# Batch 1's second FFN product in seven half products for eight

## The chip, the cores and the metric

The kernel runs on one core of a Trainium2 chip. A core has five engines with a queue of instructions each: TensorE (PE in the profile) multiplies matrices, VectorE (DVE) and ScalarE (ACT) work element by element, GpSimd (POOL) does so more slowly and issues most loads, SyncE (SP) issues stores. The metric is device time in microseconds (us) of one execution; lower is better. The median of three runs before the change is 284.22 us (284.15 to 285.25).

## The reference

Eight batches of eight heads go through an attention in which 32 global tokens see all 544 tokens and each of the 512 local tokens sees the global ones and a window of 32 to each side. The result, with the heads side by side, goes through an FFN of 512 to 2048 to 512 with a GELU (x times the sigmoid of 1.702 x).

```python
s_g = scale * np.matmul(q_g, k_all.transpose(0, 1, 3, 2))
out_g = np.matmul(sm(s_g), v_all)
mask = np.abs(pos[:, None] - pos[None, :]) <= window
s_ll = np.where(mask, scale * np.matmul(q_l, k_l.transpose(0, 1, 3, 2)), -1e9)
s_l = np.concatenate([scale * np.matmul(q_l, k_g.transpose(0, 1, 3, 2)), s_ll], axis=-1)
out_l = np.matmul(sm(s_l), np.concatenate([v_g, v_l], axis=2))
x = attn_out.transpose(0, 2, 1, 3).reshape(B * S, H * D)
h = x @ w_in
g = h * (1.0 / (1.0 + np.exp(-1.702 * h)))
return g @ w_out
```

## The kernel before

The order of the work on each engine is written out by hand: instructions go into an engine's queue in the order in which the program calls them, and each waits only for the data and the buffers that it needs. TensorE's order is the backbone. While it does the FFN of batch i it also does the attention of batch i+1 in between.

**Attention.** A quad is four heads; a batch has two, `a` and `c` (class `Wide`), and `a2`, `c2` are those of the batch after. `T` (or `Tk`, `Tq`) transposes keys and queries on VectorE, `kcopy`, `qcopy` and `ext` copy parts of them to where the score matmuls read them. `S(rnd)` are the score matmuls of one of two rounds (24 small ones), `X` the exponentials on ScalarE, `M` the multiplication with the mask, on VectorE or POOL. `U(0)` sums the rows, `U(1)` and `U(2)` multiply with the values, `Gm` does the global tokens. `R` turns the sums into reciprocals (transpose, reciprocal, transpose) and `XL` scales the result into `xL`, the FFN's input. `G`, or `keep_og`, `G_recip`, `G_mul` and `G_turn`, do the same for the global tokens.

**First product.** `h_step(i, fc)` makes one of 16 tiles of the hidden layer: four matmuls of 512 columns, then a GELU into `gT`. From batch 3 on (`h_some`) some tiles are made by `HPair` in seven products for eight.

**Second product.** For batches 0 and 1, `o_mm` adds up 16 matmuls of 512 columns for each of four tiles of 128 tokens, in sixteen parts of four matmuls. ScalarE copies each tile out of PSUM and SyncE stores it. From batch 2 on a class `Pair` does it by Strassen's scheme (in Winograd's kind): operands are cut in two along tokens, along the inner dimension and along the output, and seven products of sums of such parts stand for eight. `g_sums` makes the sums of `gT` on VectorE, `weight_sums` those of the weights (two of them in place, in `w_out_sb`). A `Pair` covers two tiles of 128 tokens; `mm(k)` is one half product of eight matmuls of 256 columns, into two PSUM banks `x` and `y`; `m3`, `z`, `zm`, `sub`, `evict`, `add` and `store` combine them:

```python
def sub(self):
    nc.vector.tensor_sub(self.zz, self.zz, self.x.rearrange("p (h m) -> p h m", h=2))
def evict(self):
    self.ob = moe.tile([128, 4, HM], F32, name="ob", bufs=3)
    on_act(self.ob[:, 1:3], self.x.rearrange("p (h m) -> p h m", h=2))
```

**PSUM.** Scores live in one pair of double banks (`spair`, `psS`, one buffer each), so `S` of a round waits until `X` has read the round before. Everything else (`hp`, `op`, `px`, `py`, `ov`, `og`) takes turns in four banks (`pbank`, `psP`).

**Loads.** Queries and keys (`load`), values (`load_v`) and the global tokens' rows (`load_g`) are issued on POOL's queue, in order with POOL's other work. Two sets of buffers hold queries and keys of two batches.

**Stages around the change.** Lines 960 to 1035: second product of batch 0 with batch 1's attention, then the start of batch 1's first product. Lines 1026 to 1054: the rest of batch 1's first product (with `weight_sums(0, 3, 4)` at 1028, and at 1029 to 1047 VectorE's work for batch 2's quads). `phase_o1` (1073 to 1114): batch 1's second product with batch 2's attention. Lines 1294 to 1318: batch 2's first product (with `weight_sums(1, 2)`). `phase_o(2)` (1116): batch 2's second product with batch 3's attention; then `h_some(3)`, `phase_o(3)` and so on.

Of the kernel before, what the change touches and what calls it, by code (L numbers as in the profile page):

```python
# [12 lines left out]
F32 = mybir.dt.float32  # L13
# [7 lines left out]
def kernel(  # L21
# [12 lines left out]
    nc = tc.nc  # L34
# [10 lines left out]
    NQ = B * 2  # L45
# [560 lines left out]
    def keep_og(q, ogs):  # L606
        on_act(ogs[:, q.u], q.st["og"][:, : D + 2])
# [69 lines left out]
    def h_weight_sums(g):  # L677
        w11, w12, w21, w22 = w_h[g]
        for t, x, y, op in zip(wh[g], (w11, w21, w11, w21, w12), (w22, w22, w12, w11, w22),
                               (ALU.add, ALU.add, ALU.add, ALU.subtract, ALU.subtract)):  # L680
            nc.vector.tensor_tensor(t, x, y, op)
# [77 lines left out]
    wsum = [wts.tile([128, FC // 2, HM], BF16, name="wsum%d" % k) if k in (0, 3, 4) else (b12, b21)[k - 1]  # L759
            for k in range(5)]  # L760

    def weight_sums(*ks):
        for k in ks:
            x, y, op = ((b11, b22, ALU.add), (b12, b22, ALU.subtract), (b21, b11, ALU.subtract),
                        (b11, b12, ALU.add), (b21, b22, ALU.add))[k]
            nc.vector.tensor_tensor(wsum[k], x, y, op)

    sums = {}

# [26 lines left out]
    class Pair:  # L796
# [37 lines left out]

        def zm(self):
            nc.vector.tensor_add(self.zz[:, 1], self.zz[:, 0], self.y[:, :HM])

        def evict(self):
            self.ob = moe.tile([128, 4, HM], F32, name="ob", bufs=3)
# [112 lines left out]
    for fc in range(4, FC):  # L952
        h_step(0, fc)
        if fc == 4:
            h_weight_sums(1)
        if fc == 12:
            h_weight_sums(2)
            h_weight_sums(4)

    def osteps(i, *sts):  # L960
        for tci, f4 in sts:
            o_mm(i, 4 * tci + f4)
# [10 lines left out]
    a.S(0)  # L973
    a.X(0)
    copy_vg1()
    c.Tk()
    c.Tq()
    c.ext()
    a.M(0)
    osteps(0, (0, 2), (1, 2))  # L980
    o_mm(0, 10, part=(0, 1))
    a.S(1)
# [40 lines left out]
    for kcs in ((0, 1), (2,), (3,)):  # L1023
        for fc in range(4):
            h_mm(1, fc, hps[fc], kcs)
    a.G()
    c.G()
    weight_sums(0, 3, 4)
    nq[2][0].Tk()
    nq[2][0].Tq()  # L1030
    transpose_g(4, 6)
    nq[2][0].ext()
    pt = spair()
    for fc in range(4, 8):
        h_mm(1, fc, bank(pt, (fc - 2) % 4), range(NKC))

    a, c = nq[2]
    for fc in range(FC):
        if fc == 11:
            c.Tk(False)  # L1040
            c.Tq(False)
            c.ext((0, 1, 2))
            c.kcopy(nc.vector.tensor_copy)
            c.ext((3,))
            c.qcopy(nc.vector.tensor_copy)
        if fc < 4:
            h_act(1, fc, hps[fc])
        elif fc in (4, 6):
            f = slice(fc, fc + 2)
            gelu(gTs[1][:, f, :], pt[1 - (fc - 4) // 2])  # L1050
        elif fc >= 8:
            h_step(1, fc)
        if fc == 13:
            a.S(0)

    def o_parts(i, *parts):
        for part in parts:
            o_mm(i, part)

    def loads_after(i):  # L1060
        if i + 2 < B:
            load_v(i + 2)
        if i == 1:
            load_g(8, NQ)
        if i + 3 < B:
            load(i + 3)

    def quads_of(n):
        if n < B and n not in nq:
# [3 lines left out]
    def phase_o1():  # L1073
        a, c = nq[2]
        a2, c2 = quads_of(3)
        a2.T()
        transpose_g(6, 8)
        a2.ext()
        a.X(0)
        a.M(0)  # L1080
        loads_after(1)
        o_parts(1, 0, 1, 2, 3, 4)
        a.S(1)
        a.X(1)
        a.M(1)
        o_parts(1, 5, 6, 7)
        c.S(0)
        c.X(0)
        a.UG()
        a.R()  # L1090
        c.M(0)
        o_parts(1, 8)
        c.S(1)
        c.X(1)
        a.XL(0)
        a.XL(1)
        a.G()
        c.M(1)
        o_parts(1, 9, 10, 11)
        a2.S(0)  # L1100
        a2.X(0)
        c.UG()
        loads_after(2)
        c.R()
        a2.M(0)
        c.XL(0)
        c.XL(1)
        o_parts(1, 12)
        a2.S(1)
        a2.X(1)  # L1110
        gelu_table()
        c.G()
        a2.M(1)
        o_parts(1, 13, 14, 15)

    def phase_o(i):
        b = i + 1
        a, c = nq[b]
        a2, c2 = quads_of(b + 1)
        p0, p1 = Pair(i, 0), Pair(i, 1)  # L1120
        ogs = att.tile([128, 2, D + 2], F32, name="ogs", bufs=1)
        late = a2 and i > 2
        exp_table()
        a.UG()
        c.S(0)
        a.R()
        g_sums(i, 7, 8, (0,))
        a.XL(0)
        wide = 2 < i < B - 1
        g_sums(i, 7, 8, (1,) if wide else (1, 2))  # L1130
        a.XL(1)
        g_sums(i, 7, 8, (3,))
        p0.mm(3, 4, 1)
        c.X(0)
        p0.m3()
        p0.z()
        if wide:
            g_sums(i, 4, 8, (2,))
# [36 lines left out]
        if a2:  # L1175
            c.XL(1)
            xg = G_mul(ogs, G_recip(ogs), nc.gpsimd)
            if i + 3 < B:
                load_v(i + 3, chunks=(2, 3, 4))
        p1.mm(3, 4)  # L1180
        p1.m3()
        p1.z()
        if c2:
            c2.Tk(False)
        else:
            c.XL(1)
# [104 lines left out]
        g_sums(i, 4, 6, (3,))  # L1291
        g_sums(i, 6, 8, (3,))

    for i in range(1, B):
        if i > 2:
            h_some(i)
        elif i > 1:
            for fc in range(FC):
                h_step(i, fc)
                if i == 2 and fc == 0:  # L1300
                    weight_sums(1, 2)
                if i + 1 < B:
                    c = nq[i + 1][1]
                    if fc == 1:
                        c.Tk()
                        c.Tq()
                        c.ext((3,))
                    if fc in (3, 5, 7):
                        c.ext(((3, 5, 7).index(fc),), on_act)
                    if fc == 9 and i + 2 < B:  # L1310
                        a2 = quads_of(i + 2)[0]
                        a2.T()
                        transpose_g(2 * i + 4, 2 * i + 6)
                        a2.ext()
                if fc in (4, 8, 12):
                    g_sums(i, fc // 2 - 2, fc // 2)
                if fc == 13:
                    g_sums(i, 6, 7)
        if i == 1:
            phase_o1()  # L1320
        elif i + 1 < B:
            phase_o(i)

    scores.close()
# [85 lines left out]
```

## Time and profile before

| what | value |
|---|---|
| median of three runs | 284.22 us |
| profiled execution's own time | 284.39 us |
| its span, first to last instruction | 282.7 us |
| TensorE's granted clock | 1.0 of full speed |
| TensorE busy | 277.0 us, 98% |
| VectorE busy | 227.6 us, 81% |
| ScalarE busy | 186.9 us, 66% |
| POOL busy | 112.3 us, 40% |

| stage (us of the span) | length | TensorE | VectorE | ScalarE | POOL |
|---|---|---|---|---|---|
| 52.86 to 65.60, batch 1, first product | 12.74 | 12.74 | 10.48 | 8.18 | 8.32 |
| 65.60 to 85.69, batch 1, second product | 20.09 | 20.09 | 15.54 | 15.71 | 14.43 |
| 85.69 to 99.51, batch 2, first product | 13.82 | 13.82 | 12.75 | 10.62 | 3.96 |
| 99.51 to 117.19, batch 2, second product | 17.68 | 17.68 | 16.25 | 11.12 | 7.24 |
| 130.61 to 148.35, batch 3, second product | 17.74 | 17.74 | 16.96 | 12.68 | 7.23 |

The profile is of one execution. A row of a timeline or of the chain of waits begins with its start and its length in us, then engine, line of the kernel, operation, and tile written <- tiles read; in brackets stands how long the engine was idle before and what ended that. PE is TensorE's matmuls, PEld its weight loads, which overlap with them. A group's row gives busy time and the mean length of one in ns; matmuls overlap in the pipeline, so their distance from start to start is less than their length. The view of waits gives, for an engine and line, what it waited for: us in total, times, longest. The chain of waits goes back from the last instruction to what released it each time.

### The profile page before, as it was taken

To read this page: it belongs to the slowest core of one execution; us is meant where nothing else is said; L and a number is where in the kernel's file an instruction comes from. 1 tells how busy PE (TensorE), PEld (TensorE's weight loads), DVE (VectorE), ACT (ScalarE), POOL (GpSimd) and SP (SyncE) were. 2 spreads that over 40 slices of the span, in tenths; PEclk is the share of its full clock that TensorE was granted. 3 is DMA by queue.
4 is the path that set the end of the run, shared out by engine and by line. 5 is a ranking of instruction groups with operands and counts; after the bars stand their busy time and mean duration, and the time that the engine had idled before them with its cause. 6 is when DMAs were issued, how large, how long until landed. Compare 5 with 4: busy or idle time off the path is not lost.

```text
span 282.7 us, 9018 instructions
## 1 busy us (share of the span) xinstructions
PE 277.0 (98%) x3787; PEld 185.5 (66%) x3787; DVE 227.6 (81%) x486; ACT 186.9 (66%) x319; POOL 112.3 (40%) x161
## 2 busy tenths in 40 slices
PE   8999999999999999999999999999999999999994
PEld 7554445544554488756886488757876589558884
DVE  7687368996689898989998899899997898586452
ACT  4847657577778785489756994689648961873331
POOL 8984550856936004970099206940080000000001
PEclk9999999999999999999999999999999999999999
DMA  7999996999999804994089807930023003300223
GB/s 207 155 191 205 204 174 84 146 218 157 165 172 175 151 2 58 93 156 90 12 108 131 148 5 91 86 70 2 20 62 74 2 2 77 74 2 1 58 54 113
DMA packets 59352, 28.24 MB, mean 100 GB/s; under 512 B 47472, under 2 KB 49776, under 8 KB 59312
## 3 DMA queue, kind: packets, MB, share of 16 engines
q0 software_dynamic: 51760, 17.83, 57.1%
q1 hardware_dynamic: 7120, 9.18, 11.8%
q8 instruction: 29, 0.48, 0.7%
q10 hardware_dynamic: 432, 0.66, 0.7%
q14 instruction: 11, 0.09, 0.1%
HBM read 36.31 MB, written 8.91 MB: 160 GB/s over the span
## 4 chain that ended last, share of the span: by engine, by line
PE 93%; DMA 2%; DVE 2%; ACT 1%; SPq 0%; issue 0%; DVEq 0%
PE hp L638 32%; PE px L821 13%; PE op L752 10%; PE py L821 9%; PE x L821 6%; PE s L560 6%; PE s L720 5%; PE ov L586 5%; PE s L638 3%; DMA early<-in_q_l_dram 2%; DVE xL L471 1%; PE og L597 1%; PE s L357 1%; ACT e L388 1%; PE s L340 1%; PE ov L438 1%
## 5 line engine op out<-in xcount | busy, mean ns | idle before, releaser
L638 PE MATMUL hp<-xL,w_in_sb 128*128 128x512 bf16 x400 | 90.1, 379 | 0.2 <-DVE xL L471 0.2
L638 PEld LDWEIGHTS <-w_in_sb 128*128 128x128 bf16 x496 | 48.2, 98 | 48.1 <-issue 0.4
L643 ACT ACTIVATE gT<-hp 128x512 bf16<-128x512 f32 x100 | 57.1, 602 | 13.4 <-PE hp L638 13.0
L571 ACT ACTIVATE e<-s 128x1016 bf16<-128x1016 f32 (+1 forms) x56 | 53.3, 1003 | 17.9 <-PE s L560 17.9
L98 POOL DMA_DIRECT2D v<-in_v_l_dram x40 | 31.0, 779 | 61.3 <-PE og L597 52.6
L821 PEld LDWEIGHTS <-gs 128*128 128x128 bf16 x480 | 46.3, 98 | 6.4
L794 DVE TENSOR_TENSOR gs<-gT 128x256 bf16<-128x256 bf16 (+2 forms) x75 | 28.2, 406 | 4.7 <-ACT gT L643 4.7
L576 POOL TENSOR_TENSOR e<-e,mask 128x1760 bf16<-128x1760 bf16 (+1 forms) x7 | 23.1, 3305 | 19.1 <-ACT e L571 19.0
L821 PE MATMUL py<-wsum,gs 128*128 128x256 bf16 x240 | 30.3, 273 | 0.0
L752 PE MATMUL op<-w_out_sb,gT 128*128 128x512 bf16 x128 | 29.5, 380 | 0.0
L854 POOL DMA_DIRECT2D out_dram<-ob x2 | 1.2, 597 | 65.1 <-ACT ob L113 64.9
L576 DVE TENSOR_TENSOR e<-e,mask 128x1712 bf16<-128x1712 bf16 (+1 forms) x21 | 22.1, 1053 | 3.3 <-ACT e L571 3.1
L512 DVE STREAM_TRANSPOSE kT<-rk 128x512 f32<-128x512 f32 x14 | 14.7, 1047 | 11.0 <-DMA rk<-in_k_l_dram 11.0
L752 PEld LDWEIGHTS <-gT 128*128 128x128 bf16 x128 | 11.8, 98 | 14.0
L821 PEld LDWEIGHTS <-gT 128*128 128x128 bf16 x192 | 18.0, 98 | 2.9
L821 PE MATMUL px<-w_out_sb,gT 128*128 128x256 bf16 x160 | 19.2, 273 | 0.0
L821 PE MATMUL px<-w_out_sb,gs 128*128 128x256 bf16 x160 | 19.1, 273 | 0.0
L471 DVE TENSOR_TENSOR xL<-ov,rs 128x512 bf16<-128x512 f32 x27 | 17.9, 686 | 0.7 <-PE ov L438 0.3
L113 ACT ACTIVATE ob<-px 128x512 f32<-128x512 f32 x10 | 6.0, 599 | 18.7 <-DVE zz L843 18.7
L560 PEld LDWEIGHTS <-kT 32*128 32x128 bf16 x672 | 12.5, 93 | 6.8 <-issue 5.3
L643 ACT ACTIVATE gT<-s 128x1024 bf16<-128x1024 f32 (+1 forms) x10 | 9.3, 938 | 11.1 <-DVE ob L734 6.6
L791 DVE TENSOR_TENSOR gs<-gT 128x1024 bf16<-128x1024 bf16 (+3 forms) x21 | 15.9, 761 | 0.0
(182 smaller groups left out, 458.8 us busy)
## 6 DMA issues: line engine op xcount, KB each, us to landing
out_dram<-ob SPq DMA_DIRECT2D x128, 64.0 KB, 2.5
rq<-in_q_l_dram POOLq DMA_DIRECT2D x5, 512.0 KB, 5.2
rk<-in_k_l_dram POOLq DMA_DIRECT2D x5, 512.0 KB, 7.9
v<-in_v_l_dram POOLq DMA_DIRECT2D x24, 96.0 KB, 4.0
w_in_sb<-in_moe_w_in_dram POOLq DMA_DIRECT2D x8, 256.0 KB, 7.8
w_out_sb<-in_moe_w_out_dram POOLq DMA_DIRECT2D x4, 512.0 KB, 10.1
rk<-in_k_l_dram POOLq DMA_DIRECT2D x5, 256.0 KB, 7.4
rq<-in_q_l_dram POOLq DMA_DIRECT2D x5, 256.0 KB, 6.9
```

The source lines that it names most:

```text
L98: nc.gpsimd.dma_start(out=vt[0:n, hs, c, :D], in_=vs[FIRST[c] : FIRST[c] + n, hs])
L471: nc.vector.tensor_mul(self.x[:, 2 * self.u + h, :], self.st[1 + h], self.st["rs"])
L512: nc.vector.transpose(flat[:, 0:Sl].rearrange("p (r t) -> p t r", t=16), loaded[self.b][0][:, self.u].bitcast(F32))
L560: nc.tensor.matmul(bank(self.ps, j)[:, at : at + n], lhsT=self.k[p, KEYS[c] : KEYS[c] + 128, e], rhs=qs[p, :, :, e], start=(e == 0), stop= ...
L571: nc.scalar.activation(self.E[rnd][:, 2 * i : 2 * i + 2, :n], self.ps[i][:, :, :n], AF.Exp, scale=scale)
L576: eng.tensor_mul(e, e, mask[:, rnd : rnd + 1, :n].to_broadcast([128, 4, n]))
L638: nc.tensor.matmul(hp[:, : width(i)], lhsT=w_in_c[:, fc // 4, kc, fc % 4 // 2, :, fc % 2], rhs=(xL[i] if i < B else xG)[:, kc, :], start=( ...
L643: nc.scalar.activation(out_, in_, AF.Gelu_apprx_sigmoid)
L752: nc.tensor.matmul(op, lhsT=gTs[i][:, fc, tci * 128 : tci * 128 + 128], rhs=w_out_sb[:, fc, :], start=(first and fc == 4 * f4), stop=(fc = ...
L791: nc.vector.tensor_tensor(sums[i][2][:, g, :n], t[:, g, 0, :n], t[:, g, 1, :n], ALU.add)
L794: nc.vector.tensor_tensor(sums[i][k][:, g, : n // 2], x[:, g], y[:, g], op)
L821: nc.tensor.matmul(out_, lhsT=lv[:, g, tt * 128 : tt * 128 + 128], rhs=rv[:, g, :], start=(g == 0 and k in ((1, 3, 4, 6) if self.apart els ...
```

## The change

Batch 1's second product is made by two `Pair`s, as for the batches after, so seven half products stand for eight. For that:

- `weight_sums(0, 3, 4)` moves from batch 1's first product to batch 0's second product, in four slices; `weight_sums(1, 2)` moves from batch 2's first product to batch 1's.
- `g_sums(1, ...)` is spread over batch 1's first product and the start of its second.
- `phase_o1` has a new order of half products, scores and attention. `a.S(0)` moves into it from the first product. `c.U` and `c.Gm` use banks again that hold `p1`'s or `a`'s results. Three masks move to POOL. Copies for batch 2's `a` and batch 3's `a2` move to ScalarE, those of batch 3's `c` to POOL (`h_two`) and ScalarE.
- Loads: `load(4)` and `load_v(4)` move from the middle of `phase_o1` to its end and behind it, `load(5)` from its end to `h_two`; `load_v(3)` is cut in two; `load_g(8, NQ)` comes earlier.
- The transposes of batch 4's first quad stay in batch 2's first product (at tile 6 for tile 9); its copies move to ScalarE in `phase_o(2)` (`late = a2`).

```diff
-    def weight_sums(*ks):
+    def weight_sums(*ks, g=slice(0, FC // 2)):
...
-            nc.vector.tensor_tensor(wsum[k], x, y, op)
+            nc.vector.tensor_tensor(wsum[k][:, g], x[:, g], y[:, g], op)
...
+    weight_sums(0, 3, 4, g=slice(2, 4))
+    weight_sums(0, 3, 4, g=slice(0, 2))
...
     copy_vg1()
+    weight_sums(0, 3, 4, g=slice(4, 6))
...
     a.M(0)
+    weight_sums(0, 3, 4, g=slice(6, 8))
...
-    a.G()
-    c.G()
-    weight_sums(0, 3, 4)
-    nq[2][0].Tk()
-    nq[2][0].Tq()
-    transpose_g(4, 6)
-    nq[2][0].ext()
+    keep_og(a, ogs)
+    keep_og(c, ogs)
+    weight_sums(1, 2)
+    GG(1, ogs)
...
+        if fc == 3:
+            g_sums(1, 0, 2)
+            a.Tk(False)
+            a.Tq(False)
+            transpose_g(4, 6)
+        if fc == 6:
+            g_sums(1, 2, 4)
+            c.Tk(False)
+            c.Tq(False)
+            c.kcopy(nc.vector.tensor_copy)
+            c.qcopy(nc.vector.tensor_copy)
+            c.ext()
+        if fc == 8:
+            a.kcopy(on_act)
+        if fc == 9:
+            a.qcopy(on_act)
+        if 10 <= fc < 14:
+            a.ext((fc - 10,), on_act)
         if fc == 13:
-            a.S(0)
+            g_sums(1, 4, 7, (0, 1))
...
     def phase_o1():
...
+        load_v(3, chunks=(0, 1))
+        load_g(8, NQ)
+        g_sums(1, 7, 8, (0, 1))
+        p0.mm(3)
+        exp_table()
+        p0.m3("dve")
+        a.S(0)
         a.X(0)
+        p0.mm(1, 6, 4)
+        g_sums(1, 4, 8, (2, 3))
+        a2.Tk(False)
+        p0.z()
+        p0.zm()
         a.S(1)
         a.X(1)
+        p0.mm(5)
+        a.M(0)
+        a2.Tq(False)
+        transpose_g(6, 8)
+        p0.mm(2)
+        p0.sub()
+        p0.evict()
         c.S(0)
         c.X(0)
+        p0.mm(7)
+        a.M(1)
+        p0.add()
+        p0.store()
+        ov = [pbank("ov"), pbank("ov")]
+        p1.mm(3)
+        p1.m3()
+        a2.kcopy(on_act)
+        a2.qcopy(on_act)
+        a.U(0, ov[0])
+        a.U(1, ov[1])
+        a.U(2)
         a.R()
         c.S(1)
         c.X(1)
+        a2.ext(copy=on_act)
+        c.M(0, nc.gpsimd)
+        load_v(3, chunks=(2, 3, 4))
         a.XL(0)
+        p1.mm(4, 1)
+        p1.z()
+        a.Gm(ov[1])
+        keep_og(a, ogs)
         a.XL(1)
         c.M(1)
+        p1.zm()
+        p1.mm(5)
         a2.S(0)
         a2.X(0)
+        a2.M(0, nc.gpsimd)
+        c.U(0, a.st[2])
         c.R()
+        p1.mm(2)
+        p1.sub()
+        p1.evict()
+        p1.mm(6)
+        a2.S(1)
+        a2.X(1)
+        c.U(1, p1.x)
+        c.U(2, a.st[2])
+        c.Gm(ov[1][:, 128:256])
+        keep_og(c, ogs)
         c.XL(0)
         c.XL(1)
+        p1.mm(7)
         gelu_table()
+        p1.add()
+        p1.store()
+        xg = G_mul(ogs, G_recip(ogs), nc.gpsimd)
+        load(4)
+        a2.M(1, nc.gpsimd)
+        return xg
+
+    def h_two(xg):
...
+        c.Tk(False)
+        c.Tq(False)
+        c.kcopy(pool)
+        c.qcopy(pool)
+        c.ext((3,), pool)
+        load_v(4)
+        load(5)
+        G_turn(2, xg)
+        for fc in range(FC):
+            h_step(2, fc)
+            if fc in (5, 7, 9):
+                c.ext(((5, 7, 9).index(fc),), on_act)
+            if fc in (4, 8, 12):
+                g_sums(2, fc // 2 - 2, fc // 2)
+            if fc == 6:
+                a2.Tk(False)
+                a2.Tq(False)
+                transpose_g(8, 10)
+            if fc == 13:
+                g_sums(2, 6, 7)
...
-        late = a2 and i > 2
+        late = a2
...
+    h_two(phase_o1())
+    phase_o(2)
+    for i in range(3, B):
+        h_some(i)
+        if i + 1 < B:
             phase_o(i)
```

More of the change, by code (lines that the diff above doesn't have):

```diff
@@ L836, in zm, with sub_zm, zm_sub @@
             nc.vector.tensor_add(self.zz[:, 1], self.zz[:, 0], self.y[:, :HM])
+        def sub_zm(self):
+            nc.vector.tensor_sub(self.zz[:, 1], self.zz[:, 0], self.x[:, HM:])
+            nc.vector.tensor_sub(self.zz[:, 0], self.zz[:, 0], self.x[:, :HM])
+        def zm_sub(self):
+            nc.vector.tensor_add(self.zz[:, 1], self.zz[:, 1], self.y[:, :HM])
         def evict(self):
@@ L1025 @@
             h_mm(1, fc, hps[fc], kcs)
-    a.G()
-    c.G()
-    weight_sums(0, 3, 4)
-    nq[2][0].Tk()
-    nq[2][0].Tq()
-    transpose_g(4, 6)
-    nq[2][0].ext()
+    ogs = att.tile([128, 2, D + 2], F32, name="ogs", bufs=1)
+    keep_og(a, ogs)
+    keep_og(c, ogs)
+    weight_sums(1, 2)
+    GG(1, ogs)
     pt = spair()
@@ L1038 @@
     for fc in range(FC):
[L1039 to L1045, printed above, removed]
         if fc < 4:
@@ L1052 @@
             h_step(1, fc)
-        if fc == 13:
-            a.S(0)
[L1056 to L1066, printed above, removed]
+        if fc == 3:
[16 more added lines that the diff above has]
+            a.ext((fc - 10,), on_act)
+        if fc == 13:
+            g_sums(1, 4, 7, (0, 1))
     def quads_of(n):
@@ L1075, in phase_o1 @@
         a2, c2 = quads_of(3)
-        a2.T()
-        transpose_g(6, 8)
-        a2.ext()
-        a.X(0)
-        a.M(0)
-        loads_after(1)
-        o_parts(1, 0, 1, 2, 3, 4)
+        p0, p1 = Pair(1, 0), Pair(1, 1)
+        ogs = att.tile([128, 2, D + 2], F32, name="ogs", bufs=1)
+        load_v(3, chunks=(0, 1))
[5 more added lines that the diff above has]
+        a.S(0)
+        a.X(0)
+        p0.mm(1, 6, 4)
+        g_sums(1, 4, 8, (2, 3))
@@ L1083, in phase_o1 @@
+        a2.Tk(False)
+        p0.z()
+        p0.zm()
         a.S(1)
         a.X(1)
-        a.M(1)
-        o_parts(1, 5, 6, 7)
+        p0.mm(5)
[5 more added lines that the diff above has]
+        p0.evict()
         c.S(0)
         c.X(0)
-        a.UG()
+        p0.mm(7)
[7 more added lines that the diff above has]
+        a2.qcopy(on_act)
@@ L1090, in phase_o1 @@
+        a.U(0, ov[0])
+        a.U(1, ov[1])
+        a.U(2)
         a.R()
-        c.M(0)
-        o_parts(1, 8)
         c.S(1)
         c.X(1)
+        a2.ext(copy=on_act)
+        c.M(0, nc.gpsimd)
+        load_v(3, chunks=(2, 3, 4))
         a.XL(0)
+        p1.mm(4, 1)
+        p1.z()
+        a.Gm(ov[1])
+        keep_og(a, ogs)
         a.XL(1)
-        a.G()
         c.M(1)
-        o_parts(1, 9, 10, 11)
+        p1.zm()
+        p1.mm(5)
         a2.S(0)
         a2.X(0)
-        c.UG()
@@ L1103, in phase_o1 @@
-        loads_after(2)
+        a2.M(0, nc.gpsimd)
+        c.U(0, a.st[2])
         c.R()
-        a2.M(0)
+        p1.mm(2)
[8 more added lines that the diff above has]
+        keep_og(c, ogs)
         c.XL(0)
         c.XL(1)
-        o_parts(1, 12)
-        a2.S(1)
-        a2.X(1)
+        p1.mm(7)
         gelu_table()
-        c.G()
-        a2.M(1)
-        o_parts(1, 13, 14, 15)
+        p1.add()
@@ new lines, in phase_o1 @@
+        p1.store()
[4 more added lines that the diff above has]
+    def h_two(xg):
+        c = nq[3][1]
+        a2 = quads_of(4)[0]
+        pool = nc.gpsimd.tensor_copy
+        c.Tk(False)
[18 more added lines that the diff above has]
+                g_sums(2, 6, 7)
@@ L1292, in h_some @@
         g_sums(i, 6, 8, (3,))
[L1294 to L1321, printed above, removed]
+    h_two(phase_o1())
[3 more added lines that the diff above has]
+        if i + 1 < B:
             phase_o(i)
```

## The prediction

> **What bounds the kernel now.** I read the page first (busy shares), then TensorE's waits, then the chain of waits, then the timelines of the other engines where the change falls.
>
> ```profile
> PE 277.0 (98%) x3787; PEld 185.5 (66%) x3787; DVE 227.6 (81%) x486; ACT 186.9 (66%) x319; POOL 112.3 (40%) x161
> ```
> ```profile
> PE w L183 <- POOL ones L159: 1.1, 1, 1.1
> PE s L340 <- ACT e L388: 0.4, 1, 0.4
> PE s L357 <- DVE q L316: 0.2, 1, 0.2
> PE hp L638 <- DVE xL L471: 0.2, 1, 0.2
> ```
> ```profile
> 65.79 4.32 PE op L752 x20
> ...
> 83.00 2.69 PE op L752 x12
> 85.69 13.81 PE hp L638 x64
> 99.51 1.20 PE ov L586 x63
> ...
> 105.72 1.75 PE px L821 x16
> ```
> TensorE is busy 98% of the span and waits 1.9 us in all, none of it after 53 us: here it is the bound, and only less TensorE work can shorten the run. Its clock is granted in full (1.000). The chain shows the stage that changes: batch 1's second product with batch 2's attention, 65.79 to 85.69 (19.90 us), then batch 2's first product (13.8), then its second, which already has the seven-product form.
>
> ```profile
> 94.88 1.04 DVE L512 STREAM_TRANSPOSE kT<-rk 128x512 f32<-128x512 f32 x1
> ...
> 97.77 0.75 DVE L794 TENSOR_TENSOR gs<-gT 128x512 bf16<-128x512 bf16 x2
> 98.44 0.68 DVE L791 TENSOR_TENSOR gs<-gT 128x1024 bf16<-128x1024 bf16 x1
> 99.04 0.82 DVE L794 TENSOR_TENSOR gs<-gT 128x512 bf16<-128x512 bf16 x3
> 99.78 0.42 DVE L791 TENSOR_TENSOR gs<-gT 128x512 bf16<-128x512 bf16 x1
> 100.11 0.28 DVE L794 TENSOR_TENSOR gs<-gT 128x256 bf16<-128x256 bf16 x1
> 100.32 0.71 DVE L462 STREAM_TRANSPOSE sT<-ov 128x512 f32<-128x512 f32 x1
> ```
> VectorE's timeline: at the start of batch 2's second product it comes from its sums straight into the transpose L462, without a gap. VectorE is the engine with the least room there.
>
> **The change, part by part.** The sum is made against the profiled execution's own time, 284.39 (span 282.7 and 1.7 around it), which lies 0.17 above the median of the runs.
>
> *Products.* 64 matmuls of 512 columns go; 112 of 256 come. In the chain 64 matmuls take 13.81 (0.216 each), 16 half ones 1.75 (0.109 each): 13.81 - 112 x 0.109 = 1.59 saved. The 48 extra weight loads (98 ns each in the page's groups) lie under the 109 ns pitch.
>
> *Order on TensorE.* A score block costs 0.57, and a change between scores and full-height products about 0.1 more (12 products after scores are 2.70 in the chain, and 12 x 0.216 = 2.59). I count five changes into products in this stage before and seven after: +0.2. Work after, from 65.22 (a score block has moved out of the first product): 14 x 0.873 + 6 x 0.57 + two sets of U and Gm at 1.37 + 7 x 0.1 = 19.08, ending at 84.30 where before it ended at 85.69. Without waits: -1.39. The Trainium skill, TensorEngine Tiling (Array Packing), Key Properties, says that a change of the tiling mode drains TensorE, which speaks against cutting the order finer. A full drain would cost what a matmul of the chain's kind lasts beyond its pitch (379 ns in the page's groups less 216), 0.16 each way: by that rule two more blocks cost 0.65 in place of 0.2, and the run ended at 284.4 as median. The row shows about a third of it, so the row stands.
>
> *New waits in that stage.* Scores share one pair of PSUM buffers, so each score block waits for the exponentials of the one before, and the blocks now come closer. a.S(1) ends at about 70.0, its X takes 1.89 (timeline of ScalarE), to 71.85; mm(5), mm(2) end at 71.7: c.S(0) waits 0.17. The larger one is c.U(1), which now goes into p1's own bank and so waits until that is evicted. The evict L113 comes behind the subtraction:
> ```profile
> 118.53 0.60 ACT L113 ACTIVATE ob<-px 128x512 f32<-128x512 f32 x1 [2.15 <-DVE zz L843]
> ```
> From c.U(0) at 79.6: 0.6 to its first transpose, R 1.67 (sT to the next instruction behind rs), subtraction 0.68, evict 0.60, hand-overs 0.1: 83.25. TensorE has mm(2), mm(6) and a2.S(1) between, 2.5, and U(0) itself 0.36: ready at 82.48. Wait 0.77. Behind the evict in ScalarE's queue stand a2.X(1), keep_og(c) and the table load, which batch 2's first GELU waits for; it has four banks of room. Stage: 84.30 + 0.17 + 0.77 = 85.24, gain 0.45. The floor is no wait (-1.39); the other end is each of the six hand-overs waiting as long as this one, 6 x 0.77 = 4.6. I stay near the counted value, because the other four come out with 0.1 to 0.6 of cover.
>
> *VectorE, ScalarE, POOL.* VectorE gets batch 1's sums (four groups of 1.61, the stretch 93.27 to 94.88) and the copies, adds and subtractions of two pairs (4.8 by L833 to L846), 11.2 in all; it gives up 3.46 of weight sums, three masks (1.05 each, to POOL at 3.3), two quads' copies (1.3 each, to ScalarE), 0.75 of copies to POOL and 0.9 of G: 10.9. mm(1) needs the last of its sums at 67.3; gelu 15 ends at 65.8 and the two sums behind it at 66.4. The twelve early weight sums (0.33 to 0.42) go into VectorE's idle stretches of 6.21, 1.93 and 0.40 + 0.71 before 45 us: nothing. If the fourth w_out part landed later than the 40.7 at which POOL's wait for it ends, a.M(1) and a.U(0) would wait with it; they have 1.9. ScalarE's added copies fall between GELUs that leave it 0.27 idle each: gelu 15 still ends at 65.8, X(0) at 69.1, a.S(1) fits.
>
> *Loads on POOL's queue.* load_v(3) is cut in two around c.M(0), load_g comes earlier, and load(4) moves from 76.00 to behind a2.M(0) and G_mul at the stage's end. By the rows: last product 85.24, add 0.69, reciprocal 0.16, G_mul about 0.5, issue at 86.65. rk landed 7.66 after the issue of rq at 123.09 with free queues, 11.4 after that at 76.00 with full ones:
> ```profile
> rq<-in_q_l_dram POOLq DMA_DIRECT2D x1, 512.0 KB, 5.2
> rk<-in_k_l_dram POOLq DMA_DIRECT2D x1, 512.0 KB, 6.9
> ```
> ```profile
> rq<-in_q_l_dram POOLq DMA_DIRECT2D x1, 512.0 KB, 8.0
> rk<-in_k_l_dram POOLq DMA_DIRECT2D x1, 512.0 KB, 10.7
> ```
> I take the free case (load_v(3) is done by then, and load_v(4) is issued later): 94.3. a2.Tk stands in VectorE's queue at fc 6 and waits for it; behind it Tq and the transposes of G (1.78 in all), sums 2:4, 4:6 (1.61 each) and 6:7 (0.94): VectorE free at 100.25, against 100.32 before, although TensorE arrives 0.45 earlier. p0.mm(3) waits for that transpose of R (slack before 0.35), p0.mm(1) for XL(0) (before: ends 102.88, matmul at 103.14, slack 0.26). So 0.28 of the 0.45 is kept. load_v(4) and load(5), now later still (about 93 and 99), have cover until 119 (a2.Tk of batch 5) and 130. The kcopy, qcopy and ext moved into batch 2's second product run so in batch 3's: that stage is 17.74 against 17.68.
>
> Sum: -1.59 + 0.20 + 0.17 + 0.77 + 0.17 = -0.28: 284.1 in the profiled execution, **283.9** as median.
>
> **The rivals.** (A) The forecast, gain small because of two hand-overs. (B) The waits are covered: R and the evict run sooner, load(4) lands by 93.9 and VectorE is ahead. For it: the same pattern with evict behind subtraction costs TensorE nothing in batch 2's stage; against it, there the next U has other banks. 284.39 - 1.39 - 0.17 = 282.8, the most that the removed work allows. (C) The late load decides, slower: landing after 94.6 holds a2.Tk, the sums and R, and TensorE loses 1:1. At 11.4 after the issue, as at 76.00, it lands at 98.05: 3.75 later, so 287.6; it breaks even at 94.6 and is slower by 0.5% from 96. For it: the issue sits behind POOL's 3.35 mask and a dependent chain of VectorE; against: the queues are free then. (D) VectorE and POOL get in each other's way.
> ```profile
> 112.64 3.35 POOL L576 TENSOR_TENSOR e<-e,mask 128x1760 bf16<-128x1760 bf16 x1
> ```
> ```profile
> 114.91 2.06 DVE L694 TENSOR_TENSOR sT<-xL 128x512 bf16<-128x512 bf16 x2
> 116.89 0.41 DVE L694 TENSOR_TENSOR xs<-xL 128x512 bf16<-128x512 bf16 x1
> ```
> The first two L694 take 2.06 where the third takes 0.41: the first ended only after POOL's mask. The same meets c.M(1) (VectorE) behind c.M(0) (POOL, about 75.1 to 78.45): c.M(1) is ready at 78.0, starts at 78.45 and ends at 79.45, and c.U(0)'s second half needs it at 79.8. Cover 0.35. Sums 0:2 of batch 2 stand behind a2.M(1) on POOL until 91.4, done 93.0, before the load lands. With c.M(0) 1.2 later (as long as sub and evict ahead of its exponentials take), 0.85 is lost: 284.8. The Trainium skill, SBUF - State Buffer, Who interferes with whom, states this as an exclusive lock: the later of the two blocks until the first ends; the trace agrees (1.72 for the blocked one by these rows).
>
> **How the numbers follow.** A 0.48, B 0.20, C 0.19, D 0.13. Half a per cent is 1.42 us, about what a measurement of this kernel can tell from no change: faster is below 282.8, slower above 285.64. B lies on the first bound: half of it, and a little of A, gives 0.12. C beyond a landing at 96 is 0.15, with the worse part of D and unseen waits 0.22. Within: 0.66. The range 282.7 to 286.2 leaves out half of B's better end and C's landing beyond 96.6, about 2 in 10; the likeliest case alone spans 283.3 to 284.6 (from half of the two waits to twice the load's).
>
> **What the changed profile would show.** Right: px and py at L821 replace op of batch 1, TensorE's busy sum falls by about 1.4; TensorE waits on ScalarE's ob at c.U(1) (L586) for 0.5 to 1; VectorE idle for DMA rk before L512 near 93 to 94; batch 2's first product from about 85.2; the stretches from batch 3's first product on as long as before. Wrong: no such wait (B); TensorE waiting for sT or XL over 1 us near 101 (C); L586 waiting for L576 (D); or stages after 130 us that grow, which I exclude.

## The result and the profile after

The changed kernel takes 285.62 us (median, 285.17 to 286.53); the kernel before took 284.48 in the same series (284.15 to 285.33). The ratio is 1.0042, with a 95% interval of 1.0032 to 1.0052. It is slower by about 1.1 us, within half a per cent, and inside the range of the prediction, but on the other side of no change from the forecast of 283.9. The profiled execution has 285.89, its span 284.2 against 282.7. All medians of this document are of runs in the chip's faster state; one run of 289.26, of the half-early kernel below, was in the slower one and is left out.

The engines' line of the page, the waits of TensorE, the chain of waits (start, duration, work) from the end of batch 1's second product to the next one, and VectorE's timeline there, all of the changed kernel:

```profile
PE 274.2 (96%) x3815; PEld 189.9 (67%) x3835; DVE 233.2 (82%) x489; ACT 190.8 (67%) x341; POOL 124.8 (44%) x168
```
```profile
PE px L821 <- DVE sT L462: 1.3, 1, 1.3
...
PE px L586 <- ACT ob L113: 0.6, 1, 0.6
PE px L821 <- DVE zz L833: 0.5, 1, 0.5
```
```profile
84.84 0.99 PE py L821 x8
85.86 0.69 DVE ob L853
...
86.70 0.40 POOL xgg L616
87.11 0.26 POOL rq L81
...
87.81 8.41 DMA rk<-in_k_l_dram
...
96.25 1.05 DVE kT L512
...
102.20 0.64 DVE sT L462
...
102.88 1.91 PE px L821 x16
```
```profile
93.41 0.61 DVE L794 TENSOR_TENSOR gs<-gT 128x512 bf16<-128x512 bf16 x1
96.25 1.05 DVE L512 STREAM_TRANSPOSE kT<-rk 128x512 f32<-128x512 f32 x1 [2.23 <-DMA rk<-in_k_l_dram]
...
101.91 0.29 DVE L794 TENSOR_TENSOR gs<-gT 128x256 bf16<-128x256 bf16 x1
102.11 0.71 DVE L462 STREAM_TRANSPOSE sT<-ov 128x512 f32<-128x512 f32 x1
```

TensorE has less to do and waits more: three waits are new from 60 us on, 2.4 us in all. The first one is the largest. Before, the chain stayed on TensorE from batch 2's first product into the second:

```profile
100.87 0.57 PE s L560 x22
101.45 1.85 PE px L821 x16
```

Now it leaves TensorE at 85.84, goes through the add of the last pair, G_mul and a DMA of 8.41 us, and then through VectorE's queue: L512, the transpose of batch 4's keys, stands there behind fc 6 and waits 2.23 for the load; sums 2:4, 4:6, 6:7 and R's transpose L462 stand behind it, 102.11 in place of 100.32. TensorE starts 1.43 later, and the end is 1.51 later. That is rival C. The first stage, which was to be 0.45 shorter, ends at 85.84 in this execution, no earlier than before.

### The profile page after: what moved, and what is told of

It is laid out like the page before. It is cut to its first block, busy times and chain, and to the rows that moved or that the text cites. A ratio compares the mean times of both kernels' runs of the same rounds, so it can differ in the third digit from the quotient of the medians.

```text
span 284.2 us, 9133 instructions
## 1 busy us (share of the span) xinstructions
PE 274.2 (96%) x3815; PEld 189.9 (67%) x3835; DVE 233.2 (82%) x489; ACT 190.8 (67%) x341; POOL 124.8 (44%) x168
## 3 DMA queue, kind: packets, MB, share of 16 engines
q1 hardware_dynamic: 7120, 9.18, 11.9%
## 4 chain that ended last, share of the span: by engine, by line
PE 67%; DMA 16%; POOL 6%; DVE 6%; issue 4%; ACT 0%; POOLq 0%
PE hp L638 20%; PE px L821 15%; PE py L821 10%; PE x L821 6%; DMA rk<-in_k_l_dram 6%; DMA rq<-in_q_l_dram 6%; PE s L720 5%; PE ov L586 4%; PE s L560 4%; DMA w_out_sb<-in_moe_w_out_dram 3%; POOL w_in_sb L260 2%; DVE gs L794 1%; DVE kT L512 1%; DVE gs L791 1%; POOL mask L225 1%
## 5 line engine op out<-in xcount | busy, mean ns | idle before, releaser
L638 PE MATMUL hp<-xL,w_in_sb 128*128 128x512 bf16 x385 | 88.5, 379 | 0.9 <-DVE xL L471 0.2
L643 ACT ACTIVATE gT<-hp 128x512 bf16<-128x512 f32 x100 | 57.1, 602 | 11.0 <-PE hp L638 10.6
L821 PEld LDWEIGHTS <-gs 128*128 128x128 bf16 x560 | 53.6, 98 | 8.3 <-issue 0.4
L576 POOL TENSOR_TENSOR e<-e,mask 128x1760 bf16<-128x1760 bf16 (+1 forms) x10 | 33.0, 3303 | 20.5 <-ACT e L571 20.3
L794 DVE TENSOR_TENSOR gs<-gT 128x256 bf16<-128x256 bf16 (+3 forms) x86 | 34.6, 434 | 5.3 <-ACT gT L643 5.3
L821 PE MATMUL py<-wsum,gs 128*128 128x256 bf16 x288 | 36.4, 273 | 0.0
L821 PE MATMUL px<-w_out_sb,gT 128*128 128x256 bf16 x192 | 23.3, 273 | 1.3 <-DVE sT L462 1.3
L821 PEld LDWEIGHTS <-gT 128*128 128x128 bf16 x224 | 21.1, 98 | 4.9 <-issue 1.3
L821 PE MATMUL px<-w_out_sb,gs 128*128 128x256 bf16 x192 | 23.1, 273 | 0.5 <-DVE zz L833 0.5
L576 DVE TENSOR_TENSOR e<-e,mask 128x1712 bf16<-128x1712 bf16 (+1 forms) x18 | 19.4, 1076 | 1.2 <-ACT e L571 0.9
L512 DVE STREAM_TRANSPOSE kT<-rk 128x512 f32<-128x512 f32 x14 | 14.7, 1047 | 6.0 <-DMA rk<-in_k_l_dram 6.0
L791 DVE TENSOR_TENSOR gs<-gT 128x1024 bf16<-128x1024 bf16 (+3 forms) x24 | 18.8, 786 | 0.0
L560 PE MATMUL s<-q,kT 32*128 32x160 bf16 (+1 forms) x448 | 14.7, 246 | 0.0
L100 POOL DMA_DIRECT2D v<-in_v_g_dram x24 | 13.9, 580 | 1.7 <-DMA rq<-in_q_l_dram 1.7
```

What stands on the lines that cost most here:

```text
L512: nc.vector.transpose(flat[:, 0:Sl].rearrange("p (r t) -> p t r", t=16), loaded[self.b][0][:, self.u].bitcast(F32))
L560: nc.tensor.matmul(bank(self.ps, j)[:, at : at + n], lhsT=self.k[p, KEYS[c] : KEYS[c] + 128, e], rhs=qs[p, :, :, e], start=(e == 0), stop= ...
L576: eng.tensor_mul(e, e, mask[:, rnd : rnd + 1, :n].to_broadcast([128, 4, n]))
L638: nc.tensor.matmul(hp[:, : width(i)], lhsT=w_in_c[:, fc // 4, kc, fc % 4 // 2, :, fc % 2], rhs=(xL[i] if i < B else xG)[:, kc, :], start=( ...
L643: nc.scalar.activation(out_, in_, AF.Gelu_apprx_sigmoid)
L791: nc.vector.tensor_tensor(sums[i][2][:, g, :n], t[:, g, 0, :n], t[:, g, 1, :n], ALU.add)
```

## Experiments

Three questions: does the late load decide, why does it land late, and where is the gain of the first stage? All runs at a glance. "Issue" and "landing" are of batch 4's rq and rk, "VectorE free" is the start of L462 near 100 (in the early load, the half early and the load ahead of a2.M(0) L462 waits 0.56 for TensorE, so VectorE is free that much sooner); the kernel before had 284.4 to 284.6 in each series.

| kernel | median us | ratio to before (95%) | issue rq | landing rk | VectorE free | wait for sT |
|---|---|---|---|---|---|---|
| changed | 285.62 | 1.0042 (1.0032, 1.0052) | 87.05 | 96.22 | 102.11 | 1.3 |
| changed, again | 285.60 | 1.0043 (1.0028, 1.0058) | 86.27 | 95.35 | 101.24 | 1.2 |
| early load | 286.33 | 1.0087 (1.0058, 1.0115) | 72.11 | 83.22 | 101.83 | 0 |
| late transposes | 284.41 | 1.0002 (0.9991, 1.0014) | 86.52 | 95.98 | 100.27 | 0 |
| no store | 284.25 | 0.9995 (0.9985, 1.0005) | 86.50 | 94.15 | 100.04 | 0 |
| product 7 first | 285.81 | 1.0059 (1.0037, 1.0080) | 88.60 | 98.02 | 103.91 | 1.8 |
| load ahead of a2.M(0) | 284.37 | 0.9996 (0.9982, 1.0011) | 82.34 | 92.85 | 99.93 | 0 |
| half early | 284.76 | 1.0015 (0.9999, 1.0030) | 72.36, 82.68 | 80.41, 88.77 | 100.22 | 0 |

### The transposes later in VectorE's queue

```diff
-            if fc == 6:
+            if fc == 9:
                 a2.Tk(False)
                 a2.Tq(False)
                 transpose_g(8, 10)
```

> The load stays where it is; only the transposes of batch 4's keys, queries and global ones move in VectorE's queue from behind fc 6 to behind fc 9, that is behind sums 2:4. Theory 1: sums 2:4 run from 94.0 to 95.6 while the load is on its way, the transposes at 96.2 to 98.0, sums 4:6 and 6:7 to 100.6: VectorE is free 1.5 earlier than in the changed kernel, 284.3 us. Theory 2: VectorE ends as late as now, 285.4 to 285.7. A theory 3, that a late load as such costs TensorE (DMA traffic), also says no change.

Measured: 284.41, 1.2 less than the changed kernel, with the load as late as before. VectorE's timeline:

```profile
94.09 0.68 DVE L791 TENSOR_TENSOR gs<-gT 128x1024 bf16<-128x1024 bf16 x1
94.69 0.41 DVE L794 TENSOR_TENSOR gs<-gT 128x512 bf16<-128x512 bf16 x1
96.01 1.06 DVE L512 STREAM_TRANSPOSE kT<-rk 128x512 f32<-128x512 f32 x1 [0.91 <-DMA rk<-in_k_l_dram]
...
100.27 0.71 DVE L462 STREAM_TRANSPOSE sT<-ov 128x512 f32<-128x512 f32 x1
```

Sums 2:4 now fill the time in which the load is on its way; L512 waits 0.91 in place of 2.23, and R begins at 100.27, as before the change. The wait for sT is gone from TensorE's list. So it was the order in VectorE's queue: theory 1. A late load as such costs nothing (theory 3 falls), and VectorE has room enough (theory 2 falls).

### Without the store of the second pair

```diff
         p1.add()
-        p1.store()
         xg = G_mul(ogs, G_recip(ogs), nc.gpsimd)
         load(4)
```

> Leaves out the store of the second pair of batch 1 (512 KB of the output are not written), nothing else. Theory A (the load lands late because these eight transfers share the DMA engines with it: about 330 KB of theirs moved between 88.5 and 96, at 208 KB per us worth 1.6 us): rk lands 7.7 us after the issue of rq instead of 9.2, at about 94.7, VectorE waits 0.7 instead of 2.2, and the time falls to about 284.3 us. Theory B (POOL's mask right behind the issue, or VectorE's sums, hold up the load): it lands 9.2 after the issue as now, 285.6 us.

Measured: 284.25. The DMA issues between 86.4 and 96.3 us (KB each, median us from issue to landing), first of the changed kernel, then without the store:

```profile
out_dram<-ob SPq DMA_DIRECT2D x8, 64.0 KB, 5.1
rq<-in_q_l_dram POOLq DMA_DIRECT2D x1, 512.0 KB, 6.1
rk<-in_k_l_dram POOLq DMA_DIRECT2D x1, 512.0 KB, 8.4
```
```profile
rq<-in_q_l_dram POOLq DMA_DIRECT2D x1, 512.0 KB, 5.2
rk<-in_k_l_dram POOLq DMA_DIRECT2D x1, 512.0 KB, 6.9
```
and VectorE's timeline without the store:
```profile
94.17 1.05 DVE L512 STREAM_TRANSPOSE kT<-rk 128x512 f32<-128x512 f32 x1 [0.70 <-DMA rk<-in_k_l_dram]
```

rk lands 7.65 us after the issue of rq (86.50 to 94.15) in place of 9.17 (87.05 to 96.22). The prediction had taken 7.66. So the queue that was called free is not: the store of p1, eight transfers of 64 KB that SP issues as soon as the same add is done, shares the DMA engines with the load. In the changed kernel its 256 packets of 2 KB start between 87.43 and 95.23 at 0.104 us each, 1.67 us of 16 engines' time, among the load's 512, which start between 88.67 and 95.70. (From 88.5 to 96 that is 0.39 MB of the store, more than the 330 KB of the expectation.) POOL's mask stands right behind the issue here too, so theory B falls. The early load shows the other side: with the load out of the way the eight transfers land after 1.7 us in place of 5.1. The Trainium skill, DMA: Bandwidth & Descriptors, Issuing engines are not separate DMA queues, says that transfers started by scalar, sync or GpSimd engine end on the same 16 DMA engines and interleave; these rows agree, and the prediction should have asked what SP had on the way.

### The load early

```diff
         load_g(8, NQ)
+        load(4)
         g_sums(1, 7, 8, (0, 1))
...
-        load(4)
         a2.M(1, nc.gpsimd)
```

> load(4) is issued at the start of batch 1's second product (about 74.5 us, behind the global queries and keys) and no longer behind G_mul. Theory 1 (the 1.3 us come from VectorE's queue standing behind the transpose of batch 4's keys until their load lands): rk lands before 86, VectorE has no gap before L512 in batch 2's first product and is free for R at about 100.0 instead of 102.1, TensorE's wait of 1.3 for sT goes, and the time falls by 1.3 to about 284.3 us, the time of the kernel before. Theory 2 (VectorE is short there with or without the load, since its sums 0:2 ran from 89.94 to 94.02 beside POOL's mask): the gap goes but the sums are still late, TensorE waits for 0.7 or more and the time stays at 285 or above.

Measured: 286.33, 0.7 more than the changed kernel; both theories missed. The wait for the load is gone, L512 starts at 94.10 without idle time, and L462 waits for TensorE, no longer TensorE for L462:

```profile
94.10 1.04 DVE L512 STREAM_TRANSPOSE kT<-rk 128x512 f32<-128x512 f32 x1
...
101.83 0.72 DVE L462 STREAM_TRANSPOSE sT<-ov 128x512 f32<-128x512 f32 x1 [0.56 <-PE ov L586]
```

But TensorE has lost time in the first stage. Its timeline there:

```profile
79.85 0.32 PE L586 MATMUL ov<-e,ones 128*32 128x128 bf16 x8
81.97 0.41 PE L586 MATMUL ov<-e,ones 128*32 128x120 bf16 x16 [1.80 <-issue]
```

It stands still for 1.80 us inside c.U(0), ahead of a matmul that waits for no semaphore. A wait named "issue" has no cause in the profile. The records of the DMA queues offer a candidate: a queue of instruction packets (16 KB each, about 1 us) runs beside the loads and stores, and one packet comes late here. Its start, counted from the first half product of the stage:

```
late transposes      75.89 - 65.07 = 10.8
no store             75.93 - 65.04 = 10.9
load ahead of a2.M(0) 76.02 - 65.36 = 10.7
changed, again       75.59 - 64.81 = 10.8
early load           79.62 - 65.28 = 14.3
```

It starts 3.5 us later than in these four, 0.55 before TensorE stops, while packets of load(4) and of a store keep the 16 DMA engines busy (76% and 28% of their time from 79.5 to 80.7, where the two overlap). In the other six traces of the changed kernel and its versions without an early load it starts 10.6 to 11.9 after the first half product; the latest three, 11.4 to 11.9, are those of the last section in which a part of batch 2's load lags. The next experiment tests whether the bytes of load(4) ahead of the packet matter.

### Half of the load early

```diff
         load_g(8, NQ)
+        load(4, (0,))
...
         a2.X(0)
+        load(4, (1,))
         a2.M(0, nc.gpsimd)
...
-        load(4)
         a2.M(1, nc.gpsimd)
```

> As the early load, but only one half of batch 4's queries and keys (512 KB) is loaded at the start of batch 1's second product; the other half is issued ahead of a2.M(0), about 82 us. Theory P (in the early load TensorE stood still because its instruction packet, due at about 76.5 us, was queued behind 1 MB of load packets and came at 79.62): with half as many bytes ahead of it the packet comes at about 78, TensorE does not run dry or stands for at most 0.3, and the time is that of a load ahead of a2.M(0) alone, about 284.2 us. Rival (it is the place of the issue in POOL's queue, or something else of that kernel): the stall of 1.8 stays, about 286 us.

Measured: the packet starts at 77.88, 12.2 after the first half product (65.65). TensorE has no wait named issue in the stage. The time is 284.76, 1.6 less than with the whole load early, though 0.4 above the load ahead of a2.M(0) alone; in the two profiles that difference is not in this stage (from the first half product to `px L821` of batch 2 it is 35.98 in both). So half of the load early does not stall TensorE: that much is shown. That the delay follows the bytes is not: 12.2 is 1.4 more than in the four traces above, but only 0.3 more than the 11.9 that occurs with no load early. Nor does every late packet stall TensorE, as the last version below shows. That the late packet holds the very instructions that TensorE stood for is argued from the times alone, and the cause of the stall stays open.

### The load one place earlier on POOL

```diff
         a2.X(0)
+        load(4)
         a2.M(0, nc.gpsimd)
...
-        load(4)
         a2.M(1, nc.gpsimd)
```

> Only load(4) moves, by one place on POOL: ahead of a2.M(0), issued at about 82 us in place of 87; product 7 and the transposes stay. It lands at about 92.5, ahead of the 94.0 at which VectorE gets to L512, so the queue holds nothing: VectorE is free at 99.4, TensorE keeps only the wait for the evict (0.6): 284.2 us, as with the late transposes; instruction packets due at 85 may come 3 us later, as in the run with product 7, without a stall. If something other than the landing delays R: above 285.

Measured: 284.37 for 284.2 expected. rk lands at 92.85, L512 starts at 92.97 with no wait, and TensorE keeps the wait for the evict alone. Three ways to take the load off VectorE's queue (other order, less traffic, earlier issue) give 284.25 to 284.41.

### Product 7 ahead of c.U(1)

```diff
         a2.X(1)
+        p1.mm(7)
         c.U(1, p1.x)
...
-        p1.mm(7)
         gelu_table()
```

> Product 7 of the second pair goes ahead of c.U(1), which waits for the evict of that pair. If the wait of 0.6 is what product 7 can cover, it goes and batch 2's first product starts 0.6 earlier, at 85.2. By theory 1 that is not worth anything here, because the transposes of batch 4's keys still wait for the load, which is issued behind c's G, no earlier than now: 285.5 to 286.0 us, with TensorE's wait for sT grown from 1.3 to about 1.9. By theory 2 (VectorE's own work decides) as well about 285.6. If it falls by 0.6 to 285.0, the load isn't what decides.

Measured: 285.81, as expected. The wait for the evict is gone from TensorE's list and the one for sT has grown:

```profile
PE px L821 <- DVE sT L462: 1.8, 1, 1.8
```

What is taken from the first stage is handed back at VectorE's queue as long as the load decides. (This profiled execution is 287.68, well above its median, and 1.4 of that is there already at 52 us; only its waits are read here, and its times in the table are that much later.)

### The changed kernel again

> The changed kernel itself once more, for a second trace of it: in its first trace one of the 16 parts of each load of batch 2 landed 1.3 to 3.3 us behind the other fifteen (rq: fifteen by 54.70, the last at 57.87), and TensorE waited 0.5 for z behind it; four of the kernels with other edits behind that point did not show this lag. If it belongs to the change, rq lands near 57.9 again and the wait for z is there; if it comes and goes between executions, rq lands near 55 and the first stage ends 0.5 earlier, at about 85.3, while the wait for sT near 101 grows towards 1.8 or stays and the time is still 285.4 to 285.9.

Measured: 285.60. rq of batch 2 lands at 54.57 and no part of it hangs behind; the wait for z is not there. From the chain of this second trace:

```profile
71.41 0.75 PE s L560 x22
...
83.00 0.55 PE px L586 x19
...
84.07 0.99 PE py L821 x8
...
87.04 8.31 DMA rk<-in_k_l_dram
...
102.00 1.91 PE px L821 x16
```

The stage ends at 85.06, and the wait for sT is still there (1.2). In the first trace the chain reaches z through a load of batch 2 that landed late:

```profile
54.19 9.26 DMA rk<-in_k_l_dram
63.47 1.05 DVE kT L512
...
70.15 0.27 DVE zz L833
70.42 0.04 issue
70.46 1.91 PE px L821 x16
```

That load came 2 us earlier here, so the 0.5 us for z belongs to that one execution; the wait behind batch 4's load is in both.

### Together: a version faster than both

With the load out of the way, product 7 should pay. Four versions have it ahead of c.U(1): with the late transposes; with these and keys ahead of queries in load(4); with both and the add behind the load's issue; and with the load ahead of a2.M(0).

```diff
-            nc.gpsimd.dma_start(out=loaded[b][1][:, s], in_=qf[b][:, s])
-            nc.gpsimd.dma_start(out=loaded[b][0][:, s], in_=kf[b][:, s])
+            for n, src in ((0, kf), (1, qf)) if b == 4 else ((1, qf), (0, kf)):
+                nc.gpsimd.dma_start(out=loaded[b][n][:, s], in_=src[b][:, s])
```
```diff
-        p1.add()
-        p1.store()
         xg = G_mul(ogs, G_recip(ogs), nc.gpsimd)
         load(4)
+        p1.add()
+        p1.store()
```

> As the run with three edits, but the queries are loaded ahead of the keys as in the changed kernel. The load decides again: rk lands at about 96.5, VectorE is free at 100.9, TensorE (ready for R's product at 100.4) waits about 1.2 for sT: 284.9 us, 0.5 more than with the transposes alone, although TensorE's own path is 0.6 shorter. If the landing does not matter any more: 283.8.

> Three edits together: the transposes of batch 4 behind fc 9 (which alone gave 284.4), product 7 of the second pair ahead of c.U(1), and in load(4) the keys ahead of the queries. Product 7 ends the first stage about 0.6 earlier on TensorE (84.7), but c's G comes 0.6 later and with it the load: rq lands at about 96.5. The keys have landed by 93.5, so L512 runs at 95 and L316 at 96.5; VectorE is free at about 99.9 (100.3 with the transposes alone). If VectorE and the load decide as the first four runs say: 0.45 below the transposes alone, 284.0 us. If product 7 is given back in full: 284.4.

> The run with three edits, and the reciprocal, G_mul and the load go ahead of the last add of the pair (0.69 on VectorE), so that the load is issued 0.6 earlier and the store that it shares the DMA engines with 0.25 later. rq lands at about 95.8, VectorE is free at 99.5, TensorE is not held: 283.8 us, 0.2 below the three edits and about 0.7 below the kernel before. If the landing no longer decides: as the three edits.

> The transposes stay behind fc 6; load(4) goes ahead of a2.M(0) on POOL (issued at about 82.8, landing at about 91), product 7 ahead of c.U(1). By the queue theory nothing is held: 283.8 us. By what the early load showed (TensorE stood 1.80 us in the middle of its L586 matmuls for no semaphore, while a 16 KB packet of the instruction queue started at 79.62 us, 3 us later than in the other runs, with load packets all around it), a load that is on its way at 85 to 88, when the next instruction packets are due, can stall TensorE again: then a wait named issue of 1 to 2 us near 86 to 90 and 285 to 286 us.

| kernel (product 7 first, and) | median us | ratio to before (95%) |
|---|---|---|
| late transposes | 283.97 | 0.9988 (0.9979, 0.9997) |
| late transposes, keys first | 283.91 | 0.9989 (0.9978, 1.0000) |
| late transposes, keys first, add later | 283.90 | 0.9984 (0.9973, 0.9994) |
| load ahead of a2.M(0) | 283.68 | 0.9979 (0.9969, 0.9990) |

The first expectation missed: 284.9 was expected with the late transposes alone. Its base was wrong: that c's G, and with it the issue of the load, comes 0.6 later had been read from the one disturbed trace of product 7. Here rq is issued at 86.40 as without product 7, rk lands at 95.48, L512 waits 0.52 for it, and TensorE is not held. So the order of keys and queries and of the add has nothing left to give; the three agree within their intervals. The expectations of the next two were met in the time (283.91 for 284.0, 283.90 for 283.8), but not for their reason, since the late transposes and product 7 alone give as much. The best is the load ahead of a2.M(0): 0.2% faster than before. Product 7 gives 0.4 to 0.7 in the medians there (284.41 to 283.97, 284.37 to 283.68; by the ratios, which allow for the two series, 0.4 and 0.5). In the traces it gives less: the wait that it covers is 0.64, one of 0.34 takes its place, since batch 2's first product now reaches c's last normalization early, and with the load ahead of a2.M(0) it takes 35.77 in place of 35.98 from the first half product to `px L821` of batch 2. From which place the rest of the medians' difference comes is not shown. This small wait is one of the two in the following row, which is of the fastest version, with the load ahead of a2.M(0); the other one lies ahead of the stage:

```profile
PE hp L638 <- DVE xL L471: 0.5, 2, 0.3
```

In this version instruction packets near 85 came late too: the next one of 16 KB starts at 89.09 and one of 8 KB at 88.62, in the changed kernel at 85.51 and 86.25. Counted from the first half product that is 3.9 and 2.7 later, about as late as in the early load, but no wait of TensorE followed.

## Why the prediction was wrong, point by point

*Products and the order on TensorE: right in kind, the work 0.33 too small.* Eight half products take 0.87, or 0.98 when they follow scores: 0.11 per change in place of 0.1. TensorE's busy sum was to fall by 1.4: the page of the changed kernel has only 3815 of its 3835 matmuls, those that have all show 275.4 to 275.9, 1.1 to 1.6 less than the 277.0 before. A set of U and Gm, now cut up by half products, is 1.20 + 0.28 = 1.48 where 1.37 was taken. The full drain by the Trainium skill, TensorEngine Tiling (Array Packing), Key Properties, was weighed at 0.16 each way; the runs show 0.11 into the products, as the row had it. What the way out costs can't be told: a block of scores takes 0.56 to 0.58 in both kernels, but in these stages none of them stands without such a change ahead of it.

*The new waits of the stage: right.* c.S(0) was to wait 0.17: the block takes 0.75 where others take 0.57, so 0.18. c.U(1) was to wait 0.77 for the evict: 0.64. The stage was to end at 85.24 in place of 85.69. With the late transposes and without the store, whose front part ran as before to within 0.07 us (rq of batch 2 issued at 50.91 and 50.87, before at 50.94), it ends at 85.30 and 85.27. That this is so close is partly luck: the first half product starts at 65.07 and 65.04 where 65.22 was taken, and from there the stage takes 20.23 where 20.02 was forecast, since the work is 0.33 longer (0.22 of it in the two sets of U and Gm) and the waits 0.12 shorter. The 85.84 of the first trace is mostly the lag of batch 2's load, with a wait of 0.47 for z, and a front part about 0.2 later.

*The load: this step failed.* "I take the free case (load_v(3) is done by then, and load_v(4) is issued later): 94.3." The issue came near the forecast (86.27 and 87.05 for 86.65), but rk landed 9.1 to 9.2 us later, not 7.66. The row at 123.09 was of a stretch in which no store was on its way any more: the last packet of one started at 123.80, the load's first at 124.57. I counted the loads on POOL's queue and left out SP's: the store of p1, which the change itself puts there, since it hangs on the same last product as G_mul and the load.

*VectorE free at 100.25: wrong by the landing.* Without the store it is 100.04, with the store 101.24 and 102.11 (for 102.11 the issue is 0.4 later than forecast as well). The gain of 0.4 in the stage became a loss: from 0.28 kept to about 1.1 lost. With the landing as the sum had it, in the run without the store, the median is 284.25 where the kernel before has 284.56 in that series: in line with the 0.28, but the interval of the ratio, 0.9985 to 1.0005, includes no change, so the size of the gain is not shown.

*Rival C, chance 0.19, is what happened, by its own law.* It set break-even at a landing of 94.6 and 1:1 beyond: 96.22 makes 284.39 + 1.62 = 286.0, and the profiled execution has 285.89; the second trace's 95.35 makes 285.1, and that execution has 285.05. Its argument against ("the queues are free then") was the false one.

*Rival D: the blocking is there and costs nothing.* POOL's masks and VectorE's rows of the changed kernel:

```profile
75.89 3.33 POOL L576 TENSOR_TENSOR e<-e,mask 128x1760 bf16<-128x1760 bf16 x1 [1.37 <-ACT e L571]
...
88.56 3.25 POOL L576 TENSOR_TENSOR e<-e,mask 128x1712 bf16<-128x1712 bf16 x1
```
```profile
78.71 1.42 DVE L576 TENSOR_TENSOR e<-e,mask 128x1712 bf16<-128x1712 bf16 x1
...
89.94 2.64 DVE L794 TENSOR_TENSOR gs<-gT 128x512 bf16<-128x512 bf16 x2 [1.50 <-ACT gT L643]
```

c.M(1) on VectorE ends 0.9 after POOL's c.M(0), and the sums that started at 89.94 only get through once a2.M(1) ends at 91.81. The first is covered: the second half of c.U(0) starts at 80.37, 0.24 later, where 0.35 was counted. The sums are done at 94.02, before the load lands. TensorE has no wait for a mask (L576) in either trace.

*Rival B* would have needed a landing by 93.9. Of the versions without a stall only those that issue the load earlier have the whole of it by then; the fastest of them, with product 7 in place of the evict's wait, comes to 283.7, where B had 282.8.

## What to carry to other kernels

When a transfer moves to the end of a stage, look for the store of the same stage: both hang on the same last results, start together and share the DMA engines, and a landing time read where nothing else was on its way is too short: here by 1.5 us, for a store of 512 KB beside a load of 1 MB. An instruction that waits for a load belongs behind the work that needs no load, since in an in-order queue the wait is charged to everything behind it; moving three lines (fc 6 to fc 9) was worth 1.2 us here. And a load may be too early as well: at the start of the stage it came with a stall of 1.8 us, ahead of a2.M(0) with none. Move it by the least that takes the wait away.

## What the runs showed of the hardware beyond what was expected

- Instruction packets travel beside the loads and can come late: one that starts 10.6 to 11.9 us after the first half product in ten traces starts at 12.2 with 512 KB of batch 4's load early and at 14.3 with 1 MB. In the latter case TensorE stood 1.80 us under the name "issue"; in the version with the load ahead of a2.M(0) and product 7 first, packets that came 3.9 and 2.7 late went with no stall. How the DMA engines take turns between the queues is not seen in the records.
- The 16 parts of one load need not land together. In the first trace of the changed kernel fifteen parts of batch 2's rq had landed at 54.70 and the last at 57.87, and in the five loads behind it the last part kept 2.0 to 2.7 us behind the others; in the second trace the whole was there at 54.57. Three of the thirteen traces show it (also product 7 first, and product 7 with the late transposes). What held that one part back is open.
